# Where the rows of an expert tile are transposed: from TensorE to VectorE, in a Fourier layer with a mixture of experts

## The chip, the cores and the metric

The kernel runs on one core of a Trainium2 chip. The time is the device time of one execution, in microseconds; the number that counts is the median of several runs. A profiled execution gives the span from its first to its last instruction and a record of every instruction. PE is TensorE (PEld its weight loads), DVE VectorE, ACT ScalarE, POOL GpSimd, and SP the engine that issues most DMAs.

## The reference

Eight batches of 2496 tokens with 256 channels go through a Fourier layer. Each of the 19968 tokens is then sent to the best of eight experts, a two-layer network of width 1024, and scaled by its gate weight.

```python
# Fourier layer (x is batch, token, channel)
X = np.fft.rfft(x, axis=1)
Yr = Xr @ w_r - Xi @ w_i + b_r
Yi = Xr @ w_i + Xi @ w_r + b_i
Y = softshrink(Yr, 0.01) + 1j * softshrink(Yi, 0.01)
x = np.fft.irfft(Y, n=2496, axis=1).reshape(19968, 256)
# mixture of experts
logits = x @ w_gate + modality_bias[modality_id]
e_idx = argmax(logits);  gate_w = softmax(logits)[e_idx]
for e in range(8):
    mask = e_idx == e
    h = np.maximum(x[mask] @ w1[e], 0.0)
    out[mask] = gate_w[mask, None] * (h @ w2[e])
```

`softshrink` stands for the two lines of the reference that pull a value towards zero by 0.01.

## The kernel before

The Fourier layer and the routing fill the first part of the span. Their result is a table `xs` in device memory, with 272 columns a row and the rows sorted by expert: columns 0 to 127 and 144 to 271 hold the 256 channels, column 128 the gate weight, column 129 the token's number. The weights lie in a table `wsp`, each split into a high and a low part (two numbers of reduced precision whose sum is the fp32 value); the products high x high, low x high and high x low are added up.

The change lies in the second part, class `Experts`. It works through `NF` = 78 full tiles of `T` = 256 rows; a table made on the chip says which rows and which expert a tile has. Among them stand five half tiles of 128 rows (`half`), which take the experts' remainders.

For a full tile i:

- `load_x` (L785) issues one DMA on SP that brings the 256 rows into `xt`, row s*128 + p to partition p. It is issued at the end of tile i - 4, into one of four buffers.
- `prep` (L796), called between the second and the third of the four groups of tile i - 1, turns the rows by four TensorE transposes (L802) into a PSUM bank `tr`, so that channels lie on partitions. ScalarE copies its high part to `xh` (L805), VectorE subtracts (L806) and gives the low part `xl`, and copies the token numbers to `ix` (L808).
- `ffn` (L811) computes the first layer in four groups p of two 128-column blocks: twelve matmuls (L826) into one bank `h`, then ScalarE's relu `hh` (L828) and VectorE's `hl` (L829). The second layer is 48 matmuls (L856) into `y`, for each half s of the rows the eight blocks f in order, and for each block `hh`, `hh`, `hl` in turn.
- `out` (L843) scales by the gate weight on ScalarE and VectorE (L848, L846), and `put` (L869) has GpSimd scatter the rows to the output.
- `load_w` (L779) brings weights for tile i + 2, 2 MB per layer; the first layer's in the middle of tile i, the second layer's at its end. It moves bytes only where tile i + 2 has another expert than tile i.

[...] The pool `ps` has two banks each for the tags `tr`, `h` and `y`; two more belong to the routing's pool `rt.ps`, which the half tiles use as well.

The order on each engine is the order in which the code is written (a manual schedule). While the first tiles run, `tick` (L921) puts the routing of the last batch between their instructions, some small VectorE operations and GpSimd scatters. On SP a DMA is issued when its buffer is free and when one of eight completion counters is free, that is, when the DMA eight places before it on that queue has landed.

Of the kernel before, what the change touches and what calls it, by code (L numbers as in the profile page):

```python
# [9 lines left out]
F32 = mybir.dt.float32  # L10
# [7 lines left out]
PSUM = bass.MemoryType.PSUM  # L18
# [13 lines left out]
GC = D + 2 * E  # L32
JE = J * E
NTOK = 8 * SEQ
T = 256
REG = NTOK + T
TH = T // 2
NF = -(-NTOK // T)
# [89 lines left out]
class Attn:  # L128


    def __init__(self, tc, I, nb):
        self.tc, self.nc, self.I, self.nb = tc, tc.nc, I, nb
# [610 lines left out]
class Experts:  # L743
    def __init__(self, ctx, tc, I, out, rt, wsp):
        self.tc, self.nc, self.out, self.rt, self.wsp = tc, tc.nc, out, rt, wsp
        pool = lambda name, bufs, **k: ctx.enter_context(
            tc.tile_pool(name=name, bufs=bufs, reuse_waits="tile", **k))
        nc = tc.nc
        wb = lambda p, i: (p.tile([128, 2, 2, F], F32R, name=f"w1_{i}"), p.tile([128, 2, 8, D], F32R, name=f"w2_{i}"))
        self.wb = [wb(pool("mw0", 1), 0)]  # L750
        self.x = pool("mx", 4)
        self.cp = pool("mc", 1)
        self.ident = self.cp.tile([128, 128], F32, name="mident")
        nc.gpsimd.memset(self.ident, 0.0)
        nc.gpsimd.affine_select(out=self.ident, in_=self.ident, compare_op=ALU.not_equal, fill=1.0, base=0,
                                pattern=[[-1, 128]], channel_multiplier=1)
        self.h = pool("mh", 2)

        pool("mp", 1).tile([128, 16], F32, name="mpad")
        self.wb.append(wb(pool("mw1", 1), 1))  # L760
        self.hf = pool("mhf", 1)
        self.hx = pool("mhx", 3)
        self.wb.append(wb(pool("mw2", 1), 2))
        self.ps = pool("mps", 2, space=PSUM)
        self.xt = {}
        self.side = iter(())

# [17 lines left out]
    def load_x(self, i):  # L785
        nc = self.nc
        r = self.reg(i, 0, E * REG)
        if i < NF:
            t = self.x.tile([128, 2, GC], F32, tag="xt", name=f"xt_{i}")
        else:  # L790
            t = self.hx.tile([128, 1, GC], F32, tag="xt", name=f"xt_{i}")
        ins = nc.sync.dma_start(t, self.rt.xs[bass.ds(r, T if i < NF else TH), :].rearrange("(s p) c -> p s c", p=128))
        self.rt.after_fence(ins)
        self.xt[i] = t

    def prep(self, i):  # L796
        nc = self.nc
        t = self.xt[i]
        ps = self.ps.tile([128, 2, T], F32, tag="tr", name=f"tr_{i}")
        for s in range(2):  # L800
            for c in range(2):
                nc.tensor.transpose(ps[:, c, s * 128:(s + 1) * 128], t[:, s, c * 144:c * 144 + 128], self.ident)  # L802
        xh = self.h.tile([128, 2, T], F32R, tag="xh", name=f"xh_{i}")
        xl = self.h.tile([128, 2, T], F32R, tag="xl", name=f"xl_{i}")
        nc.scalar.copy(xh, ps)  # L805
        nc.vector.tensor_sub(xl, ps, xh)  # L806
        ix = self.x.tile([128, 2], I32, tag="ix", name=f"ix_{i}")
        nc.vector.tensor_copy(ix, t[:, :, 129])  # L808
        return xh, xl, ix

    def ffn(self, i, xh, xl, ix, between):  # L811

        nc = self.nc
        w1, w2 = self.weights(i)
        hh = self.h.tile([128, 8, T], F32R, tag="hh", name=f"hh_{i}")
        hl = self.h.tile([128, 8, T], F32R, tag="hl", name=f"hl_{i}")
        for p in range(4):
            if p == 2:
                between()
                next(self.side, None)  # L820
            ps = self.ps.tile([128, 2, T], F32, tag="h", name=f"h_{i}_{p}")
            for q in range(2):
                f = 2 * p + q
                ops = [(lo, c, x) for lo, x in ((0, xh), (0, xl), (1, xh)) for c in range(2)]
                for n, (lo, c, x) in enumerate(ops):
                    nc.tensor.matmul(ps[:, q, :], w1[:, lo, c, f * 128:(f + 1) * 128], x[:, c, :],  # L826
                                     start=n == 0, stop=n == 5)
            nc.scalar.activation(hh[:, 2 * p:2 * p + 2, :], ps, AF.Relu)  # L828
            nc.vector.scalar_tensor_tensor(hl[:, 2 * p:2 * p + 2, :], ps, 0.0, hh[:, 2 * p:2 * p + 2, :],  # L829
                                           ALU.max, ALU.subtract)  # L830
            self.tick()
        next(self.side, None)
        if i + 2 < NF:
            self.load_w(i + 2, 0)
        y = self.ps.tile([128, 2, D], F32, tag="y", name=f"y_{i}")
        if i == NF - 1:

            y = [y[:, 0, :], self.ps.tile([128, 2, D], F32, tag="y", name=f"y_{i}_1")[:, 0, :]]
        else:
            y = [y[:, 0, :], y[:, 1, :]]  # L840
        o = self.x.tile([128, 2, D], F32, tag="o", name=f"o_{i}")

        def out(s):  # L843
            gate = self.xt[i][:, s, 128:129]
            if s:
                nc.vector.tensor_scalar_mul(o[:, s, :], y[s], gate)  # L846
            else:
                nc.scalar.mul(o[:, s, :], y[s], gate)  # L848
            self.put(ix[:, s:s + 1], o[:, s, :])

        for s in range(2):
            n = 0
            for f in range(8):
                a, l = hh[:, f, s * 128:(s + 1) * 128], hl[:, f, s * 128:(s + 1) * 128]
                for lhsT, lo in ((a, 0), (a, 1), (l, 0)):
                    nc.tensor.matmul(y[s], lhsT, w2[:, lo, f, :], start=n == 0, stop=n == 23)  # L856
                    n += 1
                if f % 4 == 3:
                    self.tick()
            if s == 0:  # L860
                next(self.side, None)
                if i == NF - 1:
                    out(0)
        if i < NF - 1:
            out(0)
        out(1)

    def put(self, ix, o):
# [6 lines left out]
    def half(self, i):  # L875

        nc, hf = self.nc, self.hf
        w1, w2 = self.weights(i)
        t = self.xt[i]
        ps = self.ps.tile([128, 2, T], F32, tag="tr", name=f"tr_{i}")  # L880
        for c in range(2):
            nc.tensor.transpose(ps[:, c, :TH], t[:, 0, c * 144:c * 144 + 128], self.ident)
        xh = hf.tile([128, 2, TH], F32R, tag="xh", name=f"xh_{i}")
        xl = hf.tile([128, 2, TH], F32R, tag="xl", name=f"xl_{i}")
        nc.scalar.copy(xh, ps[:, :, :TH])
        nc.vector.tensor_sub(xl, ps[:, :, :TH], xh)
        ix = hf.tile([128, 1], I32, tag="ix", name=f"ix_{i}")
        nc.vector.tensor_copy(ix, t[:, :, 129])
        yield
        hs = hf.tile([128, F], F32, tag="hs", name=f"hs_{i}")  # L890
        for q in range(2):
            o = slice(q * 512, (q + 1) * 512)
            ps = self.rt.ps.tile([128, 512], F32, tag="r", name=f"h_{i}_{q}")
            ops = [(lo, c, x) for lo, x in ((0, xh), (0, xl), (1, xh)) for c in range(2)]
            for n, (lo, c, x) in enumerate(ops):
                nc.tensor.matmul(ps, x[:, c, :], w1[:, lo, c, o], start=n == 0, stop=n == 5)
            nc.scalar.activation(hs[:, o], ps, AF.Relu)
        yield
        hh = hf.tile([128, 8, TH], F32R, tag="hh", name=f"hh_{i}")
        hl = hf.tile([128, 8, TH], F32R, tag="hl", name=f"hl_{i}")  # L900
        for q in range(2):
            ps = self.rt.ps.tile([128, 4, TH], F32, tag="r", name=f"ht_{i}_{q}")
            for f in range(4):
                nc.tensor.transpose(ps[:, f, :], hs[:, (4 * q + f) * 128:(4 * q + f + 1) * 128], self.ident)
            nc.scalar.copy(hh[:, 4 * q:4 * q + 4, :], ps)
            nc.vector.tensor_sub(hl[:, 4 * q:4 * q + 4, :], ps, hh[:, 4 * q:4 * q + 4, :])
        yield
        y = self.rt.ps.tile([128, 512], F32, tag="r", name=f"y_{i}")[:, :D]
        ops = [(x, lo, f) for f in range(8) for x, lo in ((hh, 0), (hh, 1), (hl, 0))]
        for n, (x, lo, f) in enumerate(ops):  # L910
            nc.tensor.matmul(y, x[:, f, :], w2[:, lo, f, :], start=n == 0, stop=n == 23)
        o = hf.tile([128, D], F32, tag="o", name=f"o_{i}")
        nc.vector.tensor_scalar_mul(o, y, t[:, 0, 128:129])
        self.put(ix, o)
# [333 lines left out]
```

## Time and profile before

| | |
|---|---|
| median of three runs | 1660.69 us (1658.56 to 1667.56) |
| profiled execution | 1657.9 us |
| its span | 1656.1 us |
| mean granted TensorE clock | 0.979 |
| expert stage | from about 714 us (first tile) to 1650 us |
| TensorE busy | 1566.3 us of the span |
| VectorE, ScalarE, GpSimd busy | 900.6, 792.0, 638.0 us |
| DMAs on the hardware queue | 101305 packets, 201.78 MB |

A row of the view in order of time has the start, the length, the engine, the line of the kernel, the operation, the tiles it writes and reads, its size, how many alike were merged (x4), and in brackets the idle time before it with what ended it. A row of one tile's instructions has the least, median and greatest length in nanoseconds. Rows of SPq are the issue of a DMA, not its transfer.

### The profile page before, as it was taken

The numbers are of one execution on the slowest core, as the hardware profiler recorded it, in microseconds if no ns is written. First come the engines' busy times: TensorE is split into PE (matmuls) and PEld (weight loads), VectorE is DVE, ScalarE is ACT, GpSimd is POOL, SyncE is SP. The second block draws the span as 40 slices with busy tenths as digits, with TensorE's granted clock in tenths as the row PEclk, the third lists the DMA queues.
The fourth block names the chain that finished last, engine by engine and source line by source line (L and its number), as shares of the span: only waits on it lengthen the run. The fifth ranks groups of instructions, "written<-read, shape, count | busy, mean of one in ns | idle before, by whom it ended". The sixth has DMA issues, their size and how long they took to land. (4 is left out here: it accounts for less than half of the span.)

```text
span 1656.1 us, 34047 instructions
## 1 busy us (share of the span) xinstructions
PE 1566.3 (95%) x12771; PEld 1522.0 (92%) x12771; DVE 900.6 (54%) x1847; ACT 792.0 (48%) x1658; POOL 638.0 (39%) x601
## 2 busy tenths in 40 slices
PE   4899989899989999999999999999999999999998
PEld 2788888798888888899999999999999999999998
DVE  3988978797979797754333333333333333333332
ACT  3678877787778776642322332323222332232232
POOL 1563767676767677621531111111111111111111
PEclk7999999999999999999999999999999999999999
DMA  7757575757475746551341411641114117515240
GB/s 204 253 165 233 163 249 160 243 162 251 150 243 161 228 141 207 173 202 40 94 129 51 158 41 41 256 147 40 53 54 145 40 54 299 202 41 219 78 151 20
DMA packets 120462, 246.18 MB, mean 149 GB/s; under 512 B 18890, under 2 KB 74262, under 8 KB 116479
## 3 DMA queue, kind: packets, MB, share of 16 engines
q1 hardware_dynamic: 101305, 201.78, 37.5%
q0 software_dynamic: 18992, 42.22, 7.6%
q8 instruction: 102, 1.67, 0.4%
q14 instruction: 63, 0.52, 0.1%
HBM read 433.83 MB, written 100.82 MB: 323 GB/s over the span
## 5 line engine op out<-in xcount | busy, mean ns | idle before, releaser
L869 POOL DMA_INDIRECT out<-o,ix x161 | 158.6, 985 | 750.9 <-ACT o L848 699.4
L856 PE MATMUL y<-w,hh 128*128 128x256 f32 x2496 | 433.6, 278 | 0.0
L826 PE MATMUL h<-xh,w 128*128 128x256 f32 x2496 | 425.6, 283 | 0.9 <-ACT xh L805 0.7
L856 PEld LDWEIGHTS y<-w,hh 128*128 128x128 f32 x2496 | 378.0, 188 | 0.4
L826 PEld LDWEIGHTS h<-xh,w 128*128 128x128 f32 x2496 | 346.0, 189 | 1.2 <-ACT xh L805 0.9
L856 PE MATMUL y<-w,hl 128*128 128x256 f32 x1248 | 346.6, 278 | 0.0
L829 DVE SCALAR_TENSOR_TENSOR hl<-h,hh 128x512 fp32r<-128x512 f32 x312 | 215.8, 692 | 230.2 <-ACT hh L828 230.1
L828 ACT ACTIVATE hh<-h 128x512 fp32r<-128x512 f32 x312 | 186.5, 598 | 272.0 <-PE h L826 272.0
L826 PE MATMUL h<-xl,w 128*128 128x256 f32 x1248 | 247.3, 280 | 0.2 <-DVE xl L806 0.2
L856 PEld LDWEIGHTS y<-w,hl 128*128 128x128 f32 x1248 | 234.4, 188 | 0.0
L846 DVE TENSOR_SCALAR o<-y,xt 128x256 f32<-128x256 f32 x78 | 37.7, 484 | 342.9 <-ACT o L848 338.6
L848 ACT ACTIVATE o<-y,xt 128x256 f32<-128x256 f32 x78 | 37.0, 474 | 360.6 <-PE y L856 360.6
L575 POOL DMA_INDIRECT xs<-x,si x176 | 180.2, 1024 | 54.8 <-issue 52.1
L826 PEld LDWEIGHTS h<-xl,w 128*128 128x128 f32 x1248 | 191.1, 189 | 0.4 <-DVE xl L806 0.4
L346 PE MATMUL mx<-wmix,Xh 128*128 128x256 f32 x1280 | 175.9, 281 | 0.0
L346 PEld LDWEIGHTS mx<-wmix,Xh 128*128 128x128 f32 x1280 | 162.0, 191 | 0.8 <-ACT mx L326 0.2
L296 POOL TENSOR_TENSOR al<-a,ah 128x512 fp32r<-128x512 f32 x80 | 109.5, 1369 | 74.5 <-ACT ah L295 48.1
L360 POOL TENSOR_TENSOR sl<-s,sh 128x512 fp32r<-128x512 f32 x77 | 100.1, 1300 | 85.3 <-ACT sh L359 72.4
L307 PE MATMUL s<-c_m,ah 128*128 128x256 f32 x320 | 83.5, 295 | 29.7 <-DVE Xl L315 10.6
L407 DVE TENSOR_TENSOR pl<-pv,ph 120x272 fp32r<-120x272 f32 x176 | 76.8, 439 | 53.4 <-ACT ph L406 46.3
L346 PE MATMUL mx<-wmix,Xl 128*128 128x256 f32 x640 | 100.2, 279 | 0.0
L307 PEld LDWEIGHTS s<-c_m,ah 128*128 128x128 f32 x320 | 61.8, 193 | 37.1 <-ACT zh L380 12.3
(199 smaller groups left out, 2830.0 us busy)
## 6 DMA issues: line engine op xcount, KB each, us to landing
w<-wsp SPq DMA_DIRECT2D x166, 2048.0 KB
xt<-xs SPq DMA_DIRECT2D x78, 272.0 KB
a<-scr SPq DMA_DIRECT2D x80, 256.0 KB
scr<-ev SPq DMA_DIRECT2D x112, 160.0 KB
x<-in_x SPq DMA_DIRECT2D x108, 156.0 KB
wr<-in_moe_w SPq DMA_DIRECT2D x64, 256.0 KB
wsp<-wh SPq DMA_DIRECT2D x64, 256.0 KB
wsp<-wl SPq DMA_DIRECT2D x64, 256.0 KB
```

The costliest lines, as they stand in the source:

```text
L296: nc.gpsimd.tensor_sub(al, at, ah)
L307: nc.tensor.matmul(o, ah[:, i, c * 128:(c + 1) * 128], mv, start=True, stop=False)
L346: self.nc.tensor.matmul(ps[i][:, i, :], t[:, 2 * i + c, o:o + 128], self.w[:, wi, c, lo, :], start=False, stop=n == len(ops) - 1, skip_gro ...
L360: eng.tensor_sub(sl, s, sh)
L407: nc.vector.tensor_sub(pl, ps[:PK, :GC], ph)
L575: i = self.nc.gpsimd.indirect_dma_start(out=self.xs, out_offset=bass.IndirectOffsetOnAxis(ap=si[:, k:k + 1], axis=0), in_=self.at.x1[:, j, ...
L826: nc.tensor.matmul(ps[:, q, :], w1[:, lo, c, f * 128:(f + 1) * 128], x[:, c, :], start=n == 0, stop=n == 5)
L828: nc.scalar.activation(hh[:, 2 * p:2 * p + 2, :], ps, AF.Relu)
L829: nc.vector.scalar_tensor_tensor(hl[:, 2 * p:2 * p + 2, :], ps, 0.0, hh[:, 2 * p:2 * p + 2, :], ALU.max, ALU.subtract)
L846: nc.vector.tensor_scalar_mul(o[:, s, :], y[s], gate)
L856: nc.tensor.matmul(y[s], lhsT, w2[:, lo, f, :], start=n == 0, stop=n == 23)
L869: ins = self.nc.gpsimd.indirect_dma_start(out=self.out, out_offset=bass.IndirectOffsetOnAxis(ap=ix, axis=0), in_=o, in_offset=None, bounds ...
```

## The change

The rows of a full tile are no longer turned by TensorE. VectorE's transpose turns each 32x32 square of a 128-partition tile in its place; to get whole rows turned, the squares must already lie in the right places. So `load_x` brings the 256 rows as squares: for each of the two channel halves c and each quarter q of 32 channels, one DMA fills the 32 partitions from 32q with eight runs of 32 channels (128 bytes) each. A ninth DMA brings gate weight and token number, two columns of 8 bytes per row. `prep` then is one VectorE transpose from `xt` to a new SBUF tile `tr` (a pool of one buffer), the copy `xh` on ScalarE, and the subtraction `xl` on GpSimd in place of VectorE. The first layer's `h` gets a pool of four banks, the former two and those of `tr`; the half tiles, which still use TensorE, take their bank for it from the routing's pool.

```diff
+        self.tr = pool("mtr", 1)
         self.ps = pool("mps", 2, space=PSUM)
+        self.hps = pool("mhps", 4, space=PSUM)
...
         if i < NF:
-            t = self.x.tile([128, 2, GC], F32, tag="xt", name=f"xt_{i}")
...
+            x = self.x.tile([128, 2 * GC], F32, tag="xt", name=f"xt_{i}")
+            t = x[:, :2 * T].rearrange("p (c s e) -> p c s e", c=2, e=32)
+            g = x[:, 2 * T:2 * T + 4].rearrange("p (s e) -> p s e", e=2)
+            rows = self.rt.xs[bass.ds(r, T), :]
+            for c in range(2):
+                for q in range(4):
+                    o = c * 144 + q * 32
+                    self.rt.after_fence(nc.sync.dma_start(
+                        t[q * 32:(q + 1) * 32, c], rows[:, o:o + 32].rearrange("(s p) e -> p s e", p=32)))
+            self.rt.after_fence(nc.sync.dma_start(g, rows[:, 128:130].rearrange("(s p) e -> p s e", p=128)))
+            self.xt[i] = x[:, :2 * T], g
+            return
...
     def prep(self, i):
         nc = self.nc
-        t = self.xt[i]
-        ps = self.ps.tile([128, 2, T], F32, tag="tr", name=f"tr_{i}")
-        for s in range(2):
-            for c in range(2):
-                nc.tensor.transpose(ps[:, c, s * 128:(s + 1) * 128], t[:, s, c * 144:c * 144 + 128], self.ident)
+        t, g = self.xt[i]
+        tr = self.tr.tile([128, 2 * T], F32, tag="tr", name=f"tr_{i}")
+        nc.vector.transpose(tr, t)
+        tr = tr.rearrange("p (c t) -> p c t", c=2)
         xh = self.h.tile([128, 2, T], F32R, tag="xh", name=f"xh_{i}")
         xl = self.h.tile([128, 2, T], F32R, tag="xl", name=f"xl_{i}")
-        nc.scalar.copy(xh, ps)
-        nc.vector.tensor_sub(xl, ps, xh)
+        nc.scalar.copy(xh, tr)
+        nc.gpsimd.tensor_sub(xl, tr, xh)
...
     def ffn(self, i, xh, xl, ix, between):
...
-            ps = self.ps.tile([128, 2, T], F32, tag="h", name=f"h_{i}_{p}")
+            ps = self.hps.tile([128, 2, T], F32, tag="h", name=f"h_{i}_{p}")
...
     def half(self, i):
...
-        ps = self.ps.tile([128, 2, T], F32, tag="tr", name=f"tr_{i}")
+        ps = self.rt.ps.tile([128, 2, T], F32, tag="r", name=f"tr_{i}")
```

How it moves instructions, at the places that the prediction speaks of. First TensorE between the second and the third group of a tile (`h_1` and `h_2`, `xh` and `xl` the tile's two parts, `w_1` its weights), before:

```order
L826 MATMUL h_1_16107<-xh_15983,w_1_11270 128x256 x4
L826 MATMUL h_1_16107<-xl_15984,w_1_11270 128x256 x2
L826 MATMUL h_1_16107<-xh_15983,w_1_11270 128x256 x2
L802 MATMUL tr_16122<-mident,xt_15800 128x128 [waits DMAHW4_49]
L802 MATMUL tr_16122<-mident,xt_15800 128x128 x3
L826 MATMUL h_2_16133<-xh_15983,w_1_11270 128x256 [waits DVE_49]
L826 MATMUL h_2_16133<-xh_15983,w_1_11270 128x256
```

and now:

```order
L838 MATMUL h_1_16297<-xh_16165,w_1_11270 128x256 x4
L838 MATMUL h_1_16297<-xl_16166,w_1_11270 128x256 x2
L838 MATMUL h_1_16297<-xh_16165,w_1_11270 128x256 x2
L838 MATMUL h_2_16320<-xh_16165,w_1_11270 128x256 [waits PE_49]
L838 MATMUL h_2_16320<-xh_16165,w_1_11270 128x256
```

The four transposes are gone, and the third group no longer waits for VectorE's reading of a bank.

Then VectorE over one tile, from the first `hl` to the scaled output `o`, before:

```order
L829 SCALAR_TENSOR_TENSOR hl_16091<-h_0_16092,hh_16090 128x512 [waits Activation_49]
L829 SCALAR_TENSOR_TENSOR hl_16091<-h_1_16107,hh_16090 128x512 [waits Activation_49]
L806 TENSOR_TENSOR xl_16128<-tr_16122,xh_16127 128x512 [waits Activation_49]
L808 CAST ix_16131<-xt_15800 128x2 [waits DMAHW4_49,DMASW2_49,DMASW1_49]
L829 SCALAR_TENSOR_TENSOR hl_16091<-h_2_16133,hh_16090 128x512 [waits Activation_49]
L829 SCALAR_TENSOR_TENSOR hl_16091<-h_3_16148,hh_16090 128x512 [waits Activation_49]
L846 TENSOR_SCALAR o_16171<-y_16170,xt_15656 128x256 [waits Activation_49]
```

and now:

```order
L841 SCALAR_TENSOR_TENSOR hl_16281<-h_0_16282,hh_16280 128x512 [waits DVE_49,Activation_49]
L841 SCALAR_TENSOR_TENSOR hl_16281<-h_1_16297,hh_16280 128x512 [waits Activation_49]
L813 STREAM_TRANSPOSE tr_16312<-xt_15972 128x512 [waits DMAHW4_49,DMAHW3_49,DMAHW5_49,DMAHW2_49,DMAHW6_49,DMAHW1_49,DMAHW7_49,DMAHW0_49,Pool_49]
L820 CAST ix_16318<-xt_15972 128x2 [waits DMAHW4_49,DMASW2_49,DMASW1_49]
L841 SCALAR_TENSOR_TENSOR hl_16281<-h_2_16320,hh_16280 128x512 [waits Activation_49]
L841 SCALAR_TENSOR_TENSOR hl_16281<-h_3_16335,hh_16280 128x512 [waits Activation_49]
L858 TENSOR_SCALAR o_16358<-y_16357,xt_15823 128x256 [waits Activation_49]
```

The transpose stands in the place of `xl`. It waits for all eight counters of SP's DMAs and for GpSimd's last reading of `tr`, where `xl` waited for ScalarE; ScalarE's `xh` now waits for it.

Last SP from one tile's second-layer weights to the next tile's first-layer weights, before:

```order
L779 DMA w_1_11271<-wsp 128x4096 [waits DMAHW4_49,DMAHW2_49,PE_49]
L769 TENSOR_LOAD t_intb
L792 ISA
L792 DMA xt_15368<-xs 128x2x272 [waits DVE_49]
L769 TENSOR_LOAD t_intb x2
L779 ISA
L779 DMA w_0_11247<-wsp 128x4096 [waits DMAHW6_49,PE_49]
```

and now, the last part of it:

```order
L799 DMA xt_13506<-xs 32x8x32 [waits DMAHW6_49]
L799 ISA
L799 DMA xt_13506<-xs 32x8x32 [waits DMAHW7_49]
L799 ISA
L799 DMA xt_13506<-xs 32x8x32 [waits DMAHW0_49]
L801 ISA
L801 DMA xt_13506<-xs 128x2x2 [waits DMAHW1_49]
L771 TENSOR_LOAD t_intb x2
L781 ISA
L781 DMA w_1_11270<-wsp 128x4096 [waits DMAHW2_49,PE_49]
```

Nine DMAs stand where one stood, each with a counter's wait of its own, ahead of the next tile's weights.

More of the change, by code (lines that the diff above doesn't have):

```diff
@@ L788, in load_x @@
         if i < NF:
-            t = self.x.tile([128, 2, GC], F32, tag="xt", name=f"xt_{i}")
-        else:
-            t = self.hx.tile([128, 1, GC], F32, tag="xt", name=f"xt_{i}")
-        ins = nc.sync.dma_start(t, self.rt.xs[bass.ds(r, T if i < NF else TH), :].rearrange("(s p) c -> p s c", p=128))
+            x = self.x.tile([128, 2 * GC], F32, tag="xt", name=f"xt_{i}")
[10 more added lines that the diff above has]
+            return
+        t = self.hx.tile([128, 1, GC], F32, tag="xt", name=f"xt_{i}")
+        ins = nc.sync.dma_start(t, self.rt.xs[bass.ds(r, TH), :].rearrange("(s p) c -> p s c", p=128))
         self.rt.after_fence(ins)
@@ L797, in prep @@
         nc = self.nc
-        t = self.xt[i]
-        ps = self.ps.tile([128, 2, T], F32, tag="tr", name=f"tr_{i}")
-        for s in range(2):
-            for c in range(2):
-                nc.tensor.transpose(ps[:, c, s * 128:(s + 1) * 128], t[:, s, c * 144:c * 144 + 128], self.ident)
+        t, g = self.xt[i]
+        tr = self.tr.tile([128, 2 * T], F32, tag="tr", name=f"tr_{i}")
+        nc.vector.transpose(tr, t)
+        tr = tr.rearrange("p (c t) -> p c t", c=2)
         xh = self.h.tile([128, 2, T], F32R, tag="xh", name=f"xh_{i}")
         xl = self.h.tile([128, 2, T], F32R, tag="xl", name=f"xl_{i}")
-        nc.scalar.copy(xh, ps)
-        nc.vector.tensor_sub(xl, ps, xh)
+        nc.scalar.copy(xh, tr)
+        nc.gpsimd.tensor_sub(xl, tr, xh)
         ix = self.x.tile([128, 2], I32, tag="ix", name=f"ix_{i}")
-        nc.vector.tensor_copy(ix, t[:, :, 129])
+        nc.vector.tensor_copy(ix, g[:, :, 1])
         return xh, xl, ix
@@ L843, in out @@
         def out(s):
-            gate = self.xt[i][:, s, 128:129]
+            gate = self.xt[i][1][:, s, 0:1]
             if s:
```

## The prediction

> **What bounds the kernel now.** I read the page first, then the busy times by stretch, then one tile in order of time.
>
> ```profile
> span 1656.1 us, 34047 instructions
> PE 1566.3 (95%) x12771; PEld 1522.0 (92%) x12771; DVE 900.6 (54%) x1847; ACT 792.0 (48%) x1658; POOL 638.0 (39%) x601
> ...
> 860.00:960.00 100.00, 100.00 (x858) 99.47 (x858) 33.17 (x61) 29.58 (x55) 15.73 (x16) 1.00 0.29 96
> 1360.00:1460.00 100.00, 100.00 (x860) 99.59 (x859) 35.69 (x65) 30.40 (x55) 17.69 (x18) 1.00 0.58 219
> ```
>
> The last two rows are stretches of the expert stage: after the stretch stand PE, PEld, DVE, ACT and POOL busy, the granted clock, the DMA share and GB/s. TensorE never idles, at clock 1.00; VectorE and ScalarE work a third of the time, GpSimd a sixth, the DMA engines 0.29 to 0.58. This stage ends when TensorE has issued its last matmul, so what leaves TensorE's queue is worth its issue time, if nothing else becomes late. One tile in order of time:
>
> ```profile
> 1202.60 0.40 PE L826 MATMUL h<-xh,w 128*128 128x256 f32 x2
> 1204.21 0.60 ACT L828 ACTIVATE hh<-h 128x512 fp32r<-128x512 f32 x1 [0.94 <-PE h L826]
> 1204.84 0.69 DVE L829 SCALAR_TENSOR_TENSOR hl<-h,hh 128x512 fp32r<-128x512 f32 x1 [1.05 <-ACT hh L828]
> 1205.43 0.60 PE L802 MATMUL tr<-mident,xt 128*128 128x128 f32 x4
> 1205.63 0.60 ACT L828 ACTIVATE hh<-h 128x512 fp32r<-128x512 f32 x1 [0.82 <-PE h L826]
> 1205.79 0.48 PE L826 MATMUL h<-xh,w 128*128 128x256 f32 x2
> 1206.12 0.58 ACT L805 CAST xh<-tr 128x512 fp32r<-128x512 f32 x1
> 1206.26 0.69 DVE L829 SCALAR_TENSOR_TENSOR hl<-h,hh 128x512 fp32r<-128x512 f32 x1 [0.73 <-ACT hh L828]
> 1207.47 0.16 DVE L808 CAST ix<-xt 128x2 int32<-128x2 f32 x1
> 1208.61 0.39 PE L856 MATMUL y<-w,hh 128*128 128x256 f32 x2
> 1214.05 0.40 PE L826 MATMUL h<-xh,w 128*128 128x256 f32 x2
> ...
> L802 PE MATMUL tr<-mident,xt x312: 269/272/273, 713.9 to 1622.9; 128*128 128x128 f32 x156
> L806 DVE TENSOR_TENSOR xl<-tr,xh x78: 678/681/691, 715.2 to 1624.0; 128x512 fp32r<-128x512 f32 x78
> ```
>
> Start to start, a tile takes 1214.05 - 1202.60 = 11.45 us: 24 first-layer matmuls in 2.83 (to 1205.43), four transposes in 0.36 (to 1205.79), 24 more in 2.82, and 48 of the second layer in 5.44. The record of 0.60 us for the four is pipelined length; they displace 0.36.
>
> **The change, part by part.**
>
> *Removed from TensorE: 312 transposes, 78 tiles x 0.36 = 28.1 us.* Tile 1 starts with a wait for its weights, which arrive when they arrive:
>
> ```profile
> 727.71 0.47 PE L826 MATMUL h<-xh,w 128*128 128x256 f32 x2 [0.19 <-DMA w<-wsp]
> ```
>
> What tile 0 and tile 1's preparation save (two times 0.36) only lengthens this wait; 76 x 0.36 = 27.4 us count. The first tile's start, too, is hidden under it.
>
> *Four banks for the first layer.* Taken out alone, the transposes would let the third group start at 1205.43, while VectorE still reads the first group's bank until 1204.84 + 0.69 = 1205.53: 0.1 us plus the handing over, per tile, some 8 us. With four banks that wait is gone; I count 0 for it.
>
> *VectorE and ScalarE: the order inside a tile.* The transpose (128x512 out of SBUF) stands where xl stood, and xl goes to GpSimd, so VectorE's count stays; but now ScalarE's xh waits for VectorE, and queued behind xh stand hh of groups 2 and 3, behind the transpose hl of groups 2 and 3, and TensorE waits for those. No transpose of VectorE is in this trace. The nearest row is 0.68 us (L806, same size); from below the 0.16 of the small cast bounds it, from above twice the row, 1.38. I take 0.69. Counted from the tile's start: hl of group 1 ends at 1206.26 + 0.69 - 1202.60 = 4.35, transpose to 5.04, xh to 5.62, hh of group 2 to 6.22, hl of group 2 to 6.94, hh and hl of group 3 to 6.82 and 7.63. The second layer now starts at 5.66 and takes 0.113 a matmul (5.44/48), three per column block, hl in the third: hl of group 2 is first needed at 5.66 + 14 x 0.113 = 7.25, of group 3 at 7.93. Margins 0.3 us each: cost 0. A transpose above about 0.98 us eats the margin. In the first half dozen tiles the routing's small VectorE operations stand in the same queue; about 0.35 us each, 2 us in all.
>
> [...]
>
> *GpSimd: one subtraction per tile.*
>
> ```profile
> L296 POOL TENSOR_TENSOR al<-a,ah x80: 1271/1316/1757, 37.0 to 676.7; 128x512 fp32r<-128x512 f32 x80
> 1203.55 0.98 POOL L869 DMA_INDIRECT out<-o,ix  x1 [9.20 <-ACT o L848]
> ```
>
> Same shape, 1.32 us. It stands behind the two output scatters, which are done 3.2 us into the tile; it runs from 5.6 to 7.0, and xl is needed when the next tile starts, at 11.1. Its cover is 4 us. Cost 0.
>
> *The loads: one DMA per tile becomes nine.* Eight carry 256 runs of 128 bytes, the ninth 256 of 8 bytes, against 256 runs of 1088 bytes. A DMA engine gets 144 runs plus 9 completions, 153 packets a tile, where it had 17. What does such a packet cost?
>
> ```profile
> DMA packets 344, 0.20 MB, mean 202 GB/s; under 512 B 211, under 2 KB 287, under 8 KB 344
> q1 hardware_dynamic: 344, 0.20, 87.1%
> ...
> DMA packets 341, 0.49 MB, mean 140 GB/s; under 512 B 33, under 2 KB 289, under 8 KB 341
> q1 hardware_dynamic: 272, 0.28, 37.3%
> ...
> DMA packets 472, 3.96 MB, mean 396 GB/s; under 512 B 49, under 2 KB 214, under 8 KB 250
> q1 hardware_dynamic: 422, 3.78, 91.8%
> ```
>
> The third pair (722 to 732 us) is the weights: 222 packets of 16 KB take some 137 of the 147 us that 16 engines spend on this queue, 0.62 us each or 38 ns a KB (16 engines move 2 MB in 4.9 us). The first pair (77 to 78 us) holds most of a load in runs of 32 bytes (the gate's weights): 0.871 x 16 = 13.9 us for 344 packets; less 200 KB x 38 ns = 7.6 leaves 18 ns per packet. So 128 bytes cost 18 + 5 = 23 ns. The second pair (1203.5 to 1207 us) is one x load as it stands: 0.373 x 56 us / 272 = 77 ns per packet of 1088 bytes. That is the upper end, 18 the lower. I take 23, because that stretch has truly small packets. Then an engine spends 3.5 us a tile (11.8 at the upper end), beside 1 us of output scatters, in 11.1 us: hidden. Each load is issued at a tile's end and used two and a quarter tiles later, 26 us of cover.
>
> Where an expert changes, two tiles in a row load 4 MB each, and SP, which has eight completion counters for its DMAs (DMAHW0 to DMAHW7 in the order), holds the seventh and eighth x load until the two weight loads ahead have landed.
>
> ```profile
> DMA  0000000000000002999603923269999999987297
> ...
> 1203.82 0.38 SPq L792 DMA_DIRECT2D xt<-xs  x1
> ...
> q1 hardware_dynamic: 25936, 73.32, 24.3%
> q0 software_dynamic: 8848, 22.39, 6.6%
> ```
>
> The first row is the DMA share from 1203.5 to 1207 in 40 slices: the x load issued at 1203.82 moves from about 1205.8, 2 us later. The last two are the queues from 760 to 1656 us: 73.3 MB less 76 x loads of 0.28, five of 0.14 and nine pads of 0.28 leave 49 MB, 23 weight loads of 2.1 MB, and 4 come before; the scatters take 0.066 x 896 = 59 us of each engine. Counted from a tile's start, the first-layer weights of the tile two ahead are issued at 6 and land at 6 + 2 + 4.9 = 13, its second-layer weights at 11.4 and 18.3. Behind these land the x loads (X of an engine's time for all nine), then the first-layer weights of the tile three ahead: 18.3 + X + 1 + 4.9, needed at 3 x 11.1 = 33.3. That holds for X up to 9 us, 59 ns a packet. At 3.5 nothing is late.
>
> *SP and the stage's first loads.*
>
> ```profile
> 72.13 1.25 SPq L279 DMA_DIRECT2D scr<-ev  x3
> ...
> 691.32 3.37 SPq L792 DMA_DIRECT2D xt<-xs  x4
> 714.21 13.31 SPq L779 DMA_DIRECT2D w<-wsp  x5
> ```
>
> Issues in a row take 0.42 us each (1.25/3). Four loads become 36: 15 us plus registers, from 691.3 to about 709, and the rings need 4 x 3.5 = 14 us beside the row scatters. The weights were issued at 714.2, behind a scatter, so SP is in time by some 5 us. Since tile 1 waits for these weights, each microsecond past 714 costs one. I count 1 us for a partial collision.
>
> *Sum.* 27.4 saved, less 2 (routing) and 1 (start) and 1 for the half tiles' weights, which share the rings: 23.4. The profiled execution took 1657.9 us (span 1656.1 and 1.8 around it): 1634.5. The three runs' median is 1660.69, 2.8 above it, the lowest 1658.56, 0.7 above; I add 1.5 and predict 1636.
>
> **The rivals.**
>
> *A: small packets cost like large ones* (slower). At 77 ns X is 11.8 us, above the 59 ns at which the expert changes become late and, with the scatters, above the tile's 11.1. The rings then set the stage: 78 x 11.8 + 27 weight loads x 4.9 + 59 us of scatters = 1112 us, against 936 from 714 to 1650: 176 more, about 1830; at 69 ns (10.6 us) 1740. For it: the present x load's 77 ns. Against it: 18 ns in the stretch with 32-byte runs, and transfers near 426 GB/s for long ones, so the 77 contains waiting that overlaps. Chance 0.14. [...]
>
> *B: only the start is late.* At 50 ns X is 7.7: the first four loads end near 691.3 + 2 + 31 + 3 (scatters) = 727, the weights behind them are 13 us late and tile 1 with them, while every later tile is covered: 1649. Chance 0.12.
>
> *C: VectorE becomes the bound.* With 1.38 us the transpose ends at 5.73, hl of group 2 at 7.66 against 7.25: a stall of 0.41 us and the handing over, 0.42 per tile, x 77 = 32 us, more than the 27 saved. That gives 1634.5 + 32 = 1666.5, some 1668 as a median. The nine conditions that the transpose waits for could add to it. For it: the margin is only 0.3 us. Against it: every 128x512 operation of VectorE here is at 0.68 or 0.69. Chance 0.12.
>
> That the change does not do what it says would show as four transposes still in TensorE's queue; the order of instructions excludes it for full tiles.
>
> **How the numbers follow.** Forecast 0.62 (1628 to 1643 by its own costs), A 0.14, B 0.12, C 0.12. Two runs of this kernel differ by up to 0.5% (8 us), which is what I call no change. Faster: the forecast and 0.10 of B, 0.72. Same: 0.02 of B, 0.09 of C, 0.01 of a mild A, 0.12. Slower: 0.13 of A and 0.03 of C, 0.16. The range reaches from the whole saving with nothing lost (1657.9 - 28.1, and 1.5 between the profiled execution and a median, less what one run varies) to C: 1627 to 1668.
>
> **What would show it.** Right: tiles 11.09 us apart, TensorE at 100 of 100 us in those stretches, transposes near 0.69 us, DMA share up by about 0.2 with no TensorE wait for it. Wrong: TensorE waits for hl (C), for w at tile 1 alone (B), or for w at every expert change and VectorE's transpose for the x loads (A).

## The result, and the profile after

The changed kernel takes 1635.05 us (median of four runs, 1632.32 to 1638.21) where the kernel before took 1659.68 beside it (four runs, 1658.56 to 1667.56): a ratio of 0.9846, 95% interval 0.9817 to 0.9875. The forecast was 1636.

The page of the changed kernel, its span, the engines and the hardware queue:

```profile
span 1630.5 us, 35891 instructions
PE 1538.1 (94%) x12459; PEld 1492.0 (92%) x12459; DVE 894.3 (55%) x1847; ACT 787.5 (48%) x1658; POOL 738.2 (45%) x679
...
q1 hardware_dynamic: 271033, 200.70, 42.3%
```

TensorE has 312 instructions and 28.2 us of busy time less, GpSimd 100 us more (its 78 subtractions), and VectorE's count is the same. The hardware queue carries 2.7 times the packets for the same bytes.

One tile in order of time (compare the tile of the prediction):

```profile
1198.46 0.40 PE L838 MATMUL h<-xh,w 128*128 128x256 f32 x2
...
1202.12 0.69 DVE L841 SCALAR_TENSOR_TENSOR hl<-h,hh 128x512 fp32r<-128x512 f32 x1 [0.66 <-ACT hh L840]
...
1202.73 0.70 DVE L813 STREAM_TRANSPOSE tr<-xt 128x512 f32<-128x512 f32 x1
...
1203.46 0.62 ACT L817 CAST xh<-tr 128x512 fp32r<-128x512 f32 x1 [1.38 <-DVE tr L813]
...
1203.99 1.08 ACT L840 ACTIVATE hh<-h 128x512 fp32r<-128x512 f32 x2
1204.12 0.40 PE L868 MATMUL y<-w,hh 128*128 128x256 f32 x2
1204.17 1.30 POOL L818 TENSOR_TENSOR xl<-tr,xh 128x512 fp32r<-128x512 f32 x1 [2.48 <-ACT xh L817]
...
1204.62 1.29 DVE L841 SCALAR_TENSOR_TENSOR hl<-h,hh 128x512 fp32r<-128x512 f32 x2 [1.13 <-ACT hh L840]
...
1205.77 0.28 PE L868 MATMUL y<-w,hl 128*128 128x256 f32 x1
...
1209.77 0.40 PE L838 MATMUL h<-xh,w 128*128 128x256 f32 x2
```

The order is the one foretold: transpose, then `xh`, and behind `xh` on ScalarE both evictions of groups 2 and 3 (merged, x2), behind the transpose both `hl`. ScalarE's 1.38 us of waiting costs nothing, because TensorE has no gap in this tile. The durations over all 78 tiles (least, median and greatest in nanoseconds):

```profile
L813 DVE STREAM_TRANSPOSE tr<-xt x78: 700/701/712, 712.2 to 1598.9; 128x512 f32<-128x512 f32 x78
L817 ACT CAST xh<-tr x78: 618/622/625, 712.9 to 1599.7; 128x512 fp32r<-128x512 f32 x78
L818 POOL TENSOR_TENSOR xl<-tr,xh x78: 1267/1297/1307, 713.6 to 1600.4; 128x512 fp32r<-128x512 f32 x78
```

The transpose takes 0.70 us: the prediction took 0.69, from the nearest row of the same size (0.68). Busy times by stretch, and TensorE's waits from 705 us on (total, times, longest):

```profile
860.00:960.00 100.00, 100.00 (x853) 99.28 (x852) 34.26 (x64) 30.43 (x56) 28.10 (x26) 1.00 0.38 96
1160.00:1260.00 100.00, 100.00 (x867) 100.00 (x867) 34.43 (x63) 29.45 (x55) 29.34 (x28) 1.00 0.32 78
1360.00:1460.00 100.00, 97.47 (x812) 96.57 (x812) 33.01 (x61) 29.08 (x53) 27.09 (x25) 0.98 0.63 206
```

```profile
PE h L838 <- DMA w<-wsp: 2.5, 1, 2.5
PE h L838 <- ACT xh L817: 1.5, 1, 1.5
PE h L838 <- POOL xl L818: 0.8, 1, 0.8
```

TensorE is still the bound nearly everywhere. The third stretch, and the three waits, hold what is new: one wait for weights near 1397 us, and two at the stage's start (before, these two were 0.7 and 0.2 us long).

**Where the 25.6 us of span went.** The first matmul of each tile, before and after, gives this account:

| | before | after | saved |
|---|---|---|---|
| start of tile 0 | 715.21 | 713.60 | 1.6 |
| tile 0 | 12.50 | 14.18 | -1.7 |
| tile 1 to the start of the last tile | 907.7 | 882.3 | 25.4 |
| from there to the end | 20.7 | 20.4 | 0.3 |

Ahead of tile 0 only the first loads and tile 0's preparation were changed, and its first matmul waited 0.8 us longer for the preparation (1.45 against 0.68); the first row is how two executions differ, for in three profiles of the changed kernel tile 0 starts at 712.4, 713.6 and 721.0. In the third row a plain tile saves 0.42 us (11.52 against 11.10 over twelve tiles), times 77 is 32.3; 4.4 of it are lost around the wait at 1397 us, 1.3 in the first seven tiles, where the routing runs beside them, and 1.2 around the half tiles.

**The wait at 1397 us.** SP's issues and TensorE there:

```profile
1362.07 9.41 SPq L799 DMA_DIRECT2D xt<-xs  x8
...
1374.78 13.14 SPq L799 DMA_DIRECT2D xt<-xs  x8
```

```profile
1397.06 0.48 PE L838 MATMUL h<-xh,w 128*128 128x256 f32 x2 [2.53 <-DMA w<-wsp]
```

Eight issues of loads take 4 us elsewhere (4.0 at 1199.68), here 9.4 and 13.1: SP waits 2.1 and 2.4 us for the weights in front to land before it issues the last of them, one issue ahead of that takes 2.0 and 5.9 us (the median is 0.33 and 0.34), and the next weights stand behind. Three tiles in a row bring new weights here, since one expert has a single tile (full tiles alternate between two sets of weights). Behind the wait the granted clock falls, to 0.50 in each half microsecond from 1399.0 to 1401.5 us:

```profile
1390.00:1400.00 10.00, 7.47 (x59) 7.29 (x58) 1.57 (x3) 1.07 (x2) 2.02 (x3) 0.93 0.95 370
1400.00:1410.00 10.00, 10.00 (x81) 10.00 (x81) 2.81 (x6) 2.44 (x5) 1.29 (x1) 0.90 0.52 123
```

0.07 and 0.10 of 10 us are 1.7 us of lost clock (3.4 at half), on top of the 2.5 of waiting: 4.2 of the account's 4.4.

**The start.** TensorE's first matmuls, and SP's issues ahead of them:

```profile
713.60 0.51 PE L838 MATMUL h<-xh,w 128*128 128x256 f32 x2 [1.45 <-ACT xh L817]
714.95 0.50 PE L838 MATMUL h<-xl,w 128*128 128x256 f32 x2 [0.84 <-POOL xl L818]
```

```profile
689.46 3.98 SPq L799 DMA_DIRECT2D xt<-xs  x8
...
710.38 0.39 SPq L801 DMA_DIRECT2D xt<-xs  x1
...
712.38 15.59 SPq L781 DMA_DIRECT2D w<-wsp  x5
```

The 36 loads are issued from 689.5 to 710.8, and the weights behind them at 712.4, not later than the 714.2 before. What tile 0 lost, it lost to its own preparation (`xl` now takes 1.3 us on GpSimd instead of 0.68 on VectorE, with nothing to hide it) and to 3.4 us at half clock behind these two waits (granted clock 0.83 from 713 to 723 us, 1.7 us lost). The clock is the larger part: in the one profile of the experiments with the same two waits and no drop behind them, tile 0 took 12.72 us.

### The profile page after: what moved, and what is told of

Same layout as the page of the kernel before. It is cut to its first block, busy times and chain, and to the rows that moved or that the text cites. A ratio compares the mean times of both kernels' runs of the same rounds, so it can differ in the third digit from the quotient of the medians.

```text
span 1630.5 us, 35891 instructions
## 1 busy us (share of the span) xinstructions
PE 1538.1 (94%) x12459; PEld 1492.0 (92%) x12459; DVE 894.3 (55%) x1847; ACT 787.5 (48%) x1658; POOL 738.2 (45%) x679
## 5 line engine op out<-in xcount | busy, mean ns | idle before, releaser
L868 PE MATMUL y<-w,hh 128*128 128x256 f32 x2496 | 438.2, 279 | 0.0
L838 PE MATMUL h<-xh,w 128*128 128x256 f32 x2496 | 408.6, 281 | 4.0 <-DMA w<-wsp 2.5
L838 PEld LDWEIGHTS h<-xh,w 128*128 128x128 f32 x2496 | 342.2, 190 | 4.4 <-issue 2.7
L841 DVE SCALAR_TENSOR_TENSOR hl<-h,hh 128x512 fp32r<-128x512 f32 x312 | 209.6, 689 | 230.5 <-ACT hh L840 229.9
L840 ACT ACTIVATE hh<-h 128x512 fp32r<-128x512 f32 x312 | 178.2, 595 | 154.6 <-PE h L838 154.6
L818 POOL TENSOR_TENSOR xl<-tr,xh 128x512 fp32r<-128x512 f32 x78 | 101.2, 1298 | 192.6 <-ACT xh L817 192.6
L817 ACT CAST xh<-tr 128x512 fp32r<-128x512 f32 x78 | 48.5, 622 | 107.8 <-DVE ix L820 102.2
```

What stands on the lines that cost most here:

```text
L818: nc.gpsimd.tensor_sub(xl, tr, xh)
```

## The experiments

The runs were spread over several chips. On two of them, called the slower chips here, the kernel before takes 1765 to 1769 us instead of 1658 to 1660, so that kernels are compared by their ratio to the kernel before on the same chip. Nearly all of the difference lies ahead of the expert stage: the first tile of the variants starts at 800 to 812 us there, against 712 to 724 on the others.

**The changed kernel again**, twice, as a control.

> The changed kernel itself, so that the variants have a partner on the same chip: 1635 us, between 1632 and 1638.

> The changed kernel itself, as a control beside the two: tiles that alternate between 10.89 and 11.31 us, a ratio of 0.986 to the kernel before, on whatever chip.

Measured: 1632.61 us, ratio 0.9859 (0.9829 to 0.9888), and 1637.77, ratio 0.9859 (0.9814 to 0.9904). The wait for weights came again (2.5 and 2.4 us, once), and so did the tiles of 10.89 and 11.31 us. The clock fell behind this wait in the first of the two and not in the second. The wait and the tiles belong to the kernel and not to one execution; the clock drop does not come every time.

**The two halves of the change, each alone.** With VectorE's transposes, but two banks for the first layer:

```diff
-        self.hps = pool("mhps", 4, space=PSUM)
+        self.hps = pool("mhps", 2, space=PSUM)
```

> The changed kernel, but the first layer's sums have two PSUM banks, as before the change (two banks lie idle). Theory: the third group of a tile then waits for VectorE's reading of the first group's bank; the third group is due 2.83 us into the tile, that reading ends at 2.93, with the handing over 0.15 us per tile, some 12 us: 1647 us, and a row TensorE h waiting for VectorE hl in nearly every tile. Rival (the banks do nothing): 1635 us and no such row.

And the kernel before with four banks, its transposes staying on TensorE:

```diff
+        self.hps = pool("mhps", 4, space=PSUM)
...
-        ps = self.ps.tile([128, 2, T], F32, tag="tr", name=f"tr_{i}")
+        ps = self.rt.ps.tile([128, 2, T], F32, tag="r", name=f"tr_{i}")
...
-            ps = self.ps.tile([128, 2, T], F32, tag="h", name=f"h_{i}_{p}")
+            ps = self.hps.tile([128, 2, T], F32, tag="h", name=f"h_{i}_{p}")
```

> The kernel before the change with only the four banks for the first layer: the rows still go through TensorE's transposes, which now take their bank from the routing's two. Theory: the banks by themselves are worth nothing while the transposes stand between the second and third group, 1659 us (1656 to 1662). Rival (the banks made the gain): 1635 to 1645 us.

Measured: with two banks 1651.93 us, ratio 0.9960 (0.9942 to 0.9978); with the banks alone 1658.22, ratio 1.0002 (0.9984 to 1.0019). The waits of the weight loads (PEld) in the kernel with two banks show the place:

```profile
PEld h L838 <- DVE hl L841: 18.7, 68, 0.3
```

In 68 tiles the third group's first weight load waits 0.27 us for VectorE to have read the first group's bank; in the changed kernel this row is missing. From the start of tile 1 to that of the last tile it takes 901.3 us against 882.3: 19.0, the 18.7 of the row. So the banks are worth nothing while the transposes stand between the groups, and three quarters of the gain once they are gone. The effects do not add up: 0.0% and 0.4% alone, 1.5% together.

**How much room VectorE has.** The transpose is issued twice:

```diff
         nc.vector.transpose(tr, t)
+        nc.vector.transpose(tr, t)
```

> VectorE's transpose of each full tile's rows is issued twice in a row, the second over the first: 0.70 us more VectorE time a tile, ahead of xh, xl and the group's hl. This measures the margin between VectorE's work and TensorE's. Theory (margin about 0.3 us, by the hl times of the prediction): a stall of 0.1 to 0.4 us in each of 78 tiles, 8 to 30 us, 1643 to 1663. Rival 1 (no margin at all): 0.70 times 78, 54 us, about 1688. Rival 2 (margin over 0.7 us): no change, 1633.

Measured: 1777.0 us on a slower chip, ratio 1.0078 (1.0051 to 1.0104), 2.2% above the changed kernel's 0.986, some 39 us (in the profile, 46 from tile 1 to the last tile). A plain tile takes 11.77 us instead of 11.10, 0.67 more. This lies between the theory's 0.1 to 0.4 and rival 1's 0.70. One tile of it (it starts at 1299.13), and the sum of this wait:

```profile
1306.09 1.29 DVE L842 SCALAR_TENSOR_TENSOR hl<-h,hh 128x512 fp32r<-128x512 f32 x2 [1.20 <-ACT hh L841]
...
1306.83 0.39 PE L869 MATMUL y<-w,hl 128*128 128x256 f32 x1 [0.22 <-DVE hl L842]
```

```profile
PEld y L869 <- DVE hl L842: 27.9, 65, 0.4
```

The `hl` of group 2 ends at 1306.09 + 0.69 = 1306.78 and TensorE goes on at 1306.83, with the matmul that would have been due at 1306.44: 0.39 us late, and the next matmul comes 0.23 behind it instead of 0.12. That is 0.50 a tile; the rest of the 0.67 comes from a longer time between matmuls, which most tiles here show from end to end (below). In the changed kernel's tile above the same `hl` ends at 1204.62 + 0.69 - 1198.46 = 6.85 us, needed at 7.31 (the matmul at 1205.77); in the next tile it ends at 6.75 and is needed at 7.04: margins of 0.46 and 0.29, so that the prediction's 0.3 is right for the tighter half. What the theory of the run had left out is the restart, 0.11 us beyond the wait in this tile, and the longer time between matmuls.

The other test of the same margin moves the subtraction back to VectorE:

```diff
-        nc.gpsimd.tensor_sub(xl, tr, xh)
+        nc.vector.tensor_sub(xl, tr, xh)
```

> The subtraction that makes xl moves from GpSimd (1.30 us in the profile of the change) to VectorE. VectorE then has about 0.6 us more to do in each tile, and group 2's xl is done by some 7.0 to 7.2 us of the tile's period, where the first layer's matmul of that group would want it at 7.25. Theory (VectorE's margin is what the prediction's rows give, 0.3 us or a little less): no new wait of TensorE, 1632 to 1635 us, and the start shorter by about 0.6 us. Rival (the margin is already used up by the evictions in VectorE's queue): each tile stalls by some 0.4 us, 78 tiles, about 1662 us.

(The expectation means group 2's `hl`, which the second layer wants.) Measured: 1755.58 us on a slower chip, ratio 0.9941 (0.9918 to 0.9963); neither theory's number. Plain tiles take 11.15 us, 0.05 more than with GpSimd, close to what the theory said. But six tiles between 883 and 974 us take 13 to 17 us each, some 25 us more together: 12.5 are TensorE's waits, 6.8 are lost to half clock behind them (granted clock 0.92 over the 85 us from 885 to 970). In them ScalarE's eviction of group 2 starts up to 4 us after its operands are there, first TensorE's row, then ScalarE's:

```profile
L868 PE MATMUL y<-w,hh 128*128 128x256 f32 x2496 | 448.8, 281 | 13.4 <-ACT hh L840 12.5
```

```profile
ACT hh L840 <- remote: 17.5, 6, 4.0
```

"Remote" means that the profile has no instruction of this core that ends the wait. GpSimd issues three or four of the routing's scatters in a row in these tiles, right behind the two of the output, and in all six ScalarE goes on 0.9 to 1.1 us after the last of them has ended. The changed kernel has the same scatters beside its tiles, with the subtraction among them, and no such wait. So the wait goes with scatters that nothing parts; whether and how they hold ScalarE stays open. Two of the ten executions took 1744 and 1745 us, so it may not come every time. That GpSimd is the better place for the subtraction is measured all the same.

**Nine loads or one.** One load of whole rows per tile, as before the change, with VectorE's transpose on whatever it brings:

```diff
-            t = x[:, :2 * T].rearrange("p (c s e) -> p c s e", c=2, e=32)
...
+            t = x.rearrange("p (s c) -> p s c", s=2)
+            g = t[:, :, 128:130]
+            self.rt.after_fence(nc.sync.dma_start(t, self.rt.xs[bass.ds(r, T), :].rearrange("(s p) c -> p s c", p=128)))
```

> The changed kernel, but each full tile's rows come in one DMA of 256 runs of 1088 bytes, as before the change, instead of nine with short runs. The squares then hold other channels than they should, so the products are formed from mixed-up channels; every transpose, copy, matmul and scatter stays. Theory (the loads are hidden, and what was won is TensorE's time): only the one wait of 2.5 us for weights and the half-speed clock after it go away, about 4 us: 1631 us, and no expert-stage wait of TensorE for a DMA. Rival 1 (short runs slow the whole stage, for example the weights behind them): 1615 to 1625 us. Rival 2 (the wait for weights has nothing to do with the loads): 1635 us with the 2.5 us wait still there.

Measured: 1631.75 us, ratio 0.9817 (0.9780 to 0.9855). The wait for weights is gone, and SP is no longer held by the loads of rows at the same place:

```profile
1374.28 5.99 SPq L781 DMA_DIRECT2D w<-wsp  x2
1380.96 0.38 SPq L795 DMA_DIRECT2D xt<-xs  x1
```

From tile 1 to the last tile it takes 877.1 us, against 882.3, 882.1 and 881.0 in the three profiles of the changed kernel: 4 to 5 us. Some 0.5 of it lies in tiles 2 and 3, the rest is the price of the wait, with its clock in the first two profiles. The ratio's interval alone could not tell this. Tile 0 takes 14.90 us with 4 loads ahead of it instead of 36, as long as in the changed kernel's third profile (14.93), so that the loads are not what makes tile 0 long.

Then the order on SP, with all nine loads kept:

```diff
-            if i + 2 < NF:
-                self.load_w(i + 2, 1)
             if i + 4 < NF:
                 self.load_x(i + 4)
+            if i + 2 < NF:
+                self.load_w(i + 2, 1)
```

> The rows of tile i+4 are asked for before the second-layer weights of tile i+2, so on SP the nine small loads no longer stand behind half a megabyte of weights. Theory (the 2.5 us wait for weights at the third loading tile in a row comes from SP being held by the x loads behind the weights): that wait and the 3.4 us at half clock behind it go, 4 us less, about 1629. Rival (the wait is the transfer time of the weights themselves): the wait stays or moves to the second layer's weights, 1632 to 1636.

(The weights of one layer are 2 MB, not the half megabyte of this text.) Measured: 1736.07 us on a slower chip, ratio 0.9854 (0.9820 to 0.9889), no gain over the changed kernel. By the profile it is a loss: 890.7 us from tile 1 to the last tile, 8.4 more. The rival was right, in its second form: the wait moved. TensorE's waits and SP's issues:

```profile
PE y L868 <- DMA w<-wsp: 6.8, 3, 3.0
```

```profile
1470.54 9.39 SPq L799 DMA_DIRECT2D xt<-xs  x8
...
1483.20 11.21 SPq L799 DMA_DIRECT2D xt<-xs  x8
```

The first layer's weights are in time, the second layer's three times late: the small loads are held behind the first layer's weights instead, and hold the second layer's. In both orders tried some weights stand behind loads that cannot be issued yet.

**The two paces of TensorE.** In the changed kernel the tiles alternate between 10.89 and 11.31 us with the same instructions. The first layer of two tiles in a row:

```profile
1210.24 0.62 PE L838 MATMUL h<-xh,w 128*128 128x256 f32 x4
1210.92 0.62 PE L838 MATMUL h<-xh,w 128*128 128x256 f32 x4
...
1221.14 0.64 PE L838 MATMUL h<-xh,w 128*128 128x256 f32 x4
1221.85 0.64 PE L838 MATMUL h<-xh,w 128*128 128x256 f32 x4
```

From one row to the next are six matmuls: 0.68 us or 113 ns each in one tile, 0.71 or 118 in the next, both at a granted clock of 1.00. Over a tile of 96 matmuls that is the 0.42 us. Four kernels tried to move this by one extra small matmul per full tile, ahead of group 2, ahead of group 0, ahead of the second layer, and ahead of its last three matmuls (the first and the last on slower chips); the first for all:

```diff
+            if p == 2:
+                nc.tensor.matmul(ps[:, 0, :32], w1[:, 0, 0, :128], xh[:, 0, :32], start=True, stop=True)
```

> One matmul of 32 columns, whose result the group's own first matmul writes over, is put ahead of group 2's first layer in each full tile. [...] Theory A (the cadence of the matmuls, 113.3 or 117.8 ns, is set by some phase between TensorE's instructions and its queue, that one more matmul shifts): the share of tiles in the slow cadence changes from one half, by up to 0.2 us a tile to either side, 1617 to 1650. Theory B (the cadence belongs to the tile's buffers or to what other engines do): tiles still alternate, 1634 to 1637.

> The same extra matmul of 32 columns, now ahead of group 0 of each full tile's first layer, where the cadence switches in the changed kernel. Theory A (the cadence follows the order of TensorE's instructions): the tiles no longer alternate between 10.9 and 11.3 us but keep one of the two, all of them: ratio to the kernel before about 0.975 if it is the fast one, 0.992 if it is the slow one. Theory B (the slow tiles belong to one of two buffers): they alternate as they did, ratio 0.986.

> The extra matmul of 32 columns ahead of each full tile's second layer instead. Theory A: the tiles no longer alternate, or switch inside the tile, at the second layer; between 0.975 and 0.992 of the kernel before. Theory B: they alternate as in the changed kernel, 0.986.

> An extra matmul that adds zeros (32 columns, 64 rows, f32) ahead of the last three matmuls of each full tile's second layer. With the extra matmul at the head of the second layer every tile ran its first layer at 113.3 ns a matmul and its second at 117.8. Theory (the cadence is a phase that an extra matmul shifts and the tile's start shifts back): now all but the last three matmuls run at 113.3, every tile takes 10.89 us and a matmul's slot of 0.1 to 0.3 us, ratio 0.978 to 0.990. Rival (the cadence does not follow such a rule): tiles of both kinds, as in the changed kernel, each 0.1 to 0.3 us longer, ratio 0.990 to 1.000.

| extra matmul | plain tiles, us | ratio (95%) |
|---|---|---|
| none | 10.89 and 11.31 in turn | 0.986 |
| ahead of group 2 | 11.41 in 45 tiles, 11.33 in 17, in long runs | 0.9891 (0.9856 to 0.9926) |
| ahead of group 0 | 11.02 and 11.42 in turn | 0.9891 (0.9847 to 0.9935) |
| ahead of the second layer | 11.22, all | 0.9902 (0.9863 to 0.9941) |
| ahead of its last three | 11.44 and 11.84 in turn | 1.0017 (0.9991 to 1.0044) |

In the third kernel of the four every tile runs its first layer at 113 ns and its second at 118. So the pace depends on the order of TensorE's instructions, and does not belong to the buffers: two of the four no longer alternate. The other half of theory B, that other engines have a part in it, is not excluded, and ahead of group 0 the tiles alternated as its theory B had said. The rule with which I went into the last run, that an extra matmul shifts the pace and the next tile's start shifts it back, failed: the tiles alternated again, each 0.54 us longer, nearly five slots of 113 ns for one matmul. And the extra matmul ahead of group 0 cost 0.11 to 0.13 us, a whole slot, with 32 columns where the others have 256. How one gets the shorter pace throughout, worth 0.21 us a tile or 16 us in all, stays open. No kernel measurably faster than the changed one, with its full computation, came out of these runs.

## Why the prediction was right, and where its steps were not

- **Transposes removed, 0.36 us a tile.** The mechanism is right, and so is the price: in all 67 plain tiles before, the four transposes displace 0.35 or 0.36 us. But a plain tile became 0.42 us shorter, so that 77 tiles are worth 32.3 us and not 27.4. The step that failed is taking the tile of 11.45 us for all. Its first layer runs at 118 ns a matmul and its second at 113 (5.44 us). The very next tile, from 1214.05 on, takes 11.75:

```profile
1216.88 0.60 PE L802 MATMUL tr<-mident,xt 128*128 128x128 f32 x4
1217.24 0.48 PE L826 MATMUL h<-xh,w 128*128 128x256 f32 x2
...
1220.15 0.40 PE L856 MATMUL y<-w,hh 128*128 128x256 f32 x2
...
1225.80 0.40 PE L826 MATMUL h<-xh,w 128*128 128x256 f32 x2
```

  Its transposes displace 0.36 us as well, but its second layer takes 5.65. Every fourth tile before is like it, and twelve average 11.52. The changed kernel has both paces in equal parts, as the tile of 11.45 had: 11.09 was foretold for the tile after, 11.10 is the mean measured. So some 5 us of the gain come from the pace, for which the prediction has no term; why the change moved it is not known.
- **Four banks, cost 0; about 8 us without them.** Cost 0 is right, 8 us was too low: 19 (two banks). The estimate took 0.1 us plus the handing over from one tile; the wait is 0.27 us.
- **VectorE's chain, margins of 0.3 us.** Right: 0.70 us for the transpose, 0.29 and 0.46 of margin, no recurring wait. Rival C fell with the 0.70; the doubled transpose shows that its mechanism is real and its price higher: 0.39 us late cost 0.50, where C had 0.42 for 0.41. (By C's own sum, 6.94 and 0.69 more, its `hl` would end at 7.63 and not 7.66.)
- **The routing beside the first tiles, 2 us.** Measured 1.3.
- **The half tiles' weights, 1 us.** Around the half tiles 1.2 us are missing, but TensorE never waited for their weights, so the cause given is not the one seen.
- **GpSimd, cost 0.** Right in steady tiles (1.30 us, done 4 us before its use); in tile 0, where nothing hides it, it is part of the loss.
- **Loads, 23 ns per packet of 128 bytes.** Too dear. The transfer records of the changed kernel give 13 ns (median; 9 for 8 bytes, 48 for 1088), below the lower bound of 18. The queue's row from 760 to 1630 us says the same from the other side:

```profile
q1 hardware_dynamic: 180432, 72.34, 32.1%
...
xt<-xs SPq DMA_DIRECT2D x568, 32.0 KB
```

  Each engine spends 0.321 x 870 = 279 us there; before it was 0.243 x 896 = 218, of which 71 loads of 16 packets and 68.3 ns (the mean of its records of 1088 bytes) are 78. That leaves 279 - 140 = 139 us for 568/8 = 71 tiles: X is 2.0 us and not 3.5, and this queue's share rises by 0.08, not by 0.2. The bound of 18 was too high because it spread the time of a stretch of 1 us over all 344 packets: by the records the 176 packets of 32 bytes took 9 ns each, and most of the time went to 76 of 1024 bytes and 53 of 2048 (93 and 85 ns in the mean). Rival A fell with it. (The prediction's window also holds 71 loads of rows and 24 of weights, not 76 and 23, which changes nothing in the sum.) Four sizes of packet in these records, 8, 128, 1088 and 16384 bytes (9, 13, 48 and 611 ns), lie near one line of 9 ns a packet and 37 ns a KB. A byte is dearer in short packets all the same.
- **"At 3.5 nothing is late" where an expert changes.** This step failed. X was even smaller, and still a wait of 2.5 us came, because the argument looked at two loading tiles in a row and here there are three. The slack of one such tile is not given back before the next: its small loads wait for its weights to land (2.1 and 2.4 us here), and the weights after them wait for the loads. One load in place of nine takes the wait away.
- **The start, 1 us for loads that collide.** Size 1.7, cause wrong: no collision (rival B fell: SP's weights left at 712.4), but the preparation of tile 0 and the clock behind it. With them the step failed that hid the first tile's start under tile 1's wait for weights: in the changed kernel tile 1 waits for none.
- **The sum.** 23.4 foretold; measured 25.4 from tile 1 on and 0.3 at the end less 1.7 in tile 0, 24.0. The terms erred in both directions (4.9 gained by the pace, 4.2 lost at the expert change, neither counted), and part of the good fit is luck.

## What to carry to other kernels

What a loop costs on the engine that sets the time is read from a mean over a dozen of its repetitions, since neighbours with the same instructions differed by 4% here (10.89 and 11.31 us); the time that the four transposes displace was the same in all of them here. When work that separated two users of a buffer leaves the queue, plan the buffer with it: here transposes and banks were worth 0.4% and nothing alone, 1.5% together. When one load becomes many on a queue that also carries large ones, follow the issue order through the longest run of large loads that the data can bring, not through the usual one.

## What the runs showed of the hardware that was not expected

- The same matmuls, at full granted clock and without a wait, follow each other at 113 or at 118 ns, and one more instruction in the queue changed which. The mechanism is not known from these runs.
- In some profiles a wait of TensorE for weights was followed by 3.4 us at half clock (a granted clock of 0.50). Over all kernels it came behind waits of 1.74, 1.89, 1.94, 2.53, 2.54 and 2.91 us, and 6.8 us of it with one of 2.98; it did not come behind 0.84, 1.62, 1.91, 2.27, 2.41 and 2.70. So the length of the wait alone does not decide, and what else does is not shown. At the start it is the same: with the same waits of 1.5 and 0.8 us, tile 0 took 12.72 us where no drop came (the extra matmul ahead of group 2), 14.18 with 3.4 us of it, and 14.93 with 6.8 (the changed kernel's third profile).
- Short packets were cheap on these loads, counted by the packet: 13 ns for 128 bytes, against 48 for 1088.
